# An earlier place for a bank's copy, and a pair's rounding in two pieces, in LSH attention with two feed-forward layers

## Chip, cores and metric

The kernel runs on one core of a Trainium2 chip. The metric is device time in microseconds (us) of one execution. The core has five engines that are used here: TensorE (PE, matmuls, with the weight loads shown apart as PEld), VectorE (DVE), ScalarE (ACT), GpSimd (POOL) and SyncE (SP, which issues DMAs). Each works through its own list of instructions in order and waits on semaphores for the others.

## What is computed

The input is q, k and v of 2 batches, 8 heads, 768 positions and 64 dimensions. Attention is masked by a hash: only positions whose six projection signs agree see each other. Two feed-forward layers follow. Cut to what matters:

```python
mask = q_bucket[:, :, :, None] == k_bucket[:, :, None, :]
scores = np.where(mask, scale * (q @ k.T), -1e9)
attn = exp(scores - scores.max(-1)) / sum
x = (attn @ v)                                   # (1536 tokens, 512)
x = (1/(1+exp(-(x @ w_gate))) * (x @ w_val)) @ w_out
h = x @ w_in2; y = (h * cos(h)) @ w_out2
```

## The kernel before, in words

Precision is kept by splitting: a value is rounded (the high part) and what the rounding left is subtracted out (the low part); matmuls run on the parts in turn.

The attention runs over 96 steps `g` (16 heads of 6 row tiles of 128 rows), plus nine steps in which the pipeline empties. In step `g` PE makes the scores of tile g+2 (`scores`, L451 and L454), DVE the row extremum of tile g+1 (`rowmax`, L462), ACT the exponential of tile g with its row sum (`expo`, L469), and POOL normalises tile g-3 (`norm`, L502). Seven steps behind (`LAG`), P is transposed on PE in blocks of three 128x128 (`ptrans`, L518), two blocks a step, called a and b. ACT rounds each block (`phi`, L523, orders HIa and HIb), DVE subtracts (`plo`, L528, LOa and LOb), and PE multiplies both parts with the values (`pv`, L538 with the high part, L539 with the low one). Six blocks fill one output bank `o`: a group `u`, half a head. There is one bank `o`, so the first `pv` of a new group waits until ACT has copied the bank out (`fin_act`, L548). Group u ends in step g = 3u + 10; at such a step the a block's `pv` (PVaF) stands late in the list.

Every third step `coef` makes the reciprocals of three tiles' row sums on DVE (L495), which `norm` uses. At the odd steps after a head's transposes its parts `x` pass through ACT (L301) and POOL (L302, L305). The values are split on POOL, too (`values`, L265, L268).

After the copy, DMAs on SP bring the halves of the output to their partitions (L550 to L562). For every pair of heads (u = 3, 7, ... 27, and at the end u = 30 and 31) POOL sums them three steps later (`fin_sum`, L575), and five steps later ACT rounds the sum into `xy` (`fin_hi`, L591) and POOL subtracts (`fin_lo`, L595). `xy` is held in tiles of 512 tokens, so the 768 tokens of a pair fall into two pieces: 512 and 256 in the first batch, 256 and 512 in the second.

Within a step, the order of work on all engines is written out by hand in `ORDER` (L21): each name stands for one operation, and each engine's list is what of the names falls to it. FIN is the end of a group (`finish_group`, L710: the copy, its DMAs and the entries for the later steps), PREP runs what is entered for this step (`run_todo`: loads, transposes of a coming head, `bits`, values, `fin_sum`, `fin_hi`, `fin_lo`), LATE what the step before left, W the first weights of the feed-forward part (from step 72), S the scores. In the last steps the order is the same list with COEF and NRM first (`LAST`). Behind the attention stand the matmuls of the feed-forward layers (L789, L851, L878).

Of the kernel before, what the change touches and what calls it, by code (L numbers as in the profile page):

```python
# [18 lines left out]
P = 128  # L19

ORDER = (  # L21
    "Tb LOa COEF NRM PVb EXP Ta MIN LATE W HIb PVa PREP S FIN HIa PVaF LOb".split()
)
LAST = ["COEF", "NRM"] + [name for name in ORDER if name not in ("COEF", "NRM")]
FILL = "COEF NRM MIN EXP LATE W PREP S".split()
# [6 lines left out]
SUM_AT, HIGH_AT, LOW_AT = 3, 5, 5  # L32
# [8 lines left out]
def lsh_attention_glu_moe_cos_moe(  # L41
# [14 lines left out]
    B, H, S, D = q.shape  # L56
# [5 lines left out]
    NH = B * H  # L62
# [164 lines left out]
    def attention():  # L227
        nonlocal done
        parts = None
        with ExitStack() as st:  # L230
# [10 lines left out]
            NG = NH * T  # L241
# [3 lines left out]
            def load(hd, nm, t0=0, t1=T, eng=nc.sync):  # L245
                b, h = divmod(hd, H)
                if nm == "v":
                    raw[hd, "v"] = nat.tile([P, 2, T * D], F32, tag="nv", name=f"nv{hd}", bufs=1)
                    nc.sync.dma_start(
                        raw[hd, "v"], v[b, h : h + 2].rearrange("h (p t) d -> p h (t d)", p=P)  # L250
                    )
                    return
                if hd not in raw:
                    raw[hd] = nat.tile([P, T, 2 * D], F32, tag="nqk", name=f"nqk{hd}")
                i = "qk".index(nm)
                eng.dma_start(
                    raw[hd][:, t0:t1, i * D : (i + 1) * D],
                    (q, k)[i][b, h].rearrange("(p t) d -> p t d", p=P)[:, t0:t1, :],
                )
# [304 lines left out]
            def fin_cols(u):  # L564
                if u // 2 < NH - 1:
                    return 0, S
                return u % 2 * HS, (u % 2 + 1) * HS

            def fin_engine(u):
                return nc.vector if u == 2 * NH - 1 else nc.gpsimd  # L570
# [6 lines left out]
            def pieces(u):  # L577
                b, h = divmod(u // 2, H)
                lo, hi = (b * S + c for c in fin_cols(u))
                c0 = lo  # L580
                while c0 < hi:
                    c, o = divmod(c0, 512)
                    n = min(512 - o, hi - c0)
                    yield xy[c][:, 0, h // 2, o : o + n], xy[c][:, 1, h // 2, o : o + n], f_t[u // 4][
                        :, c0 - b * S : c0 - b * S + n
                    ]
                    c0 += n

            def fin_hi(u):
                for h, _, x in pieces(u):  # L590
                    nc.scalar.copy(h, x)  # L591

            def fin_lo(u):
                for h, lw, x in pieces(u):
                    fin_engine(u).tensor_tensor(out=lw, in0=x, in1=h.bitcast(F32), op=ALU.subtract)  # L595

            LAG = 7
# [7 lines left out]
            def at(step, fn):  # L605
                todo.setdefault(step, []).append(fn)
# [42 lines left out]
            def run_todo(step):  # L649
                for fn in todo.pop(step, []):  # L650
                    e = fn()
                    if e is not None:
                        late.append(e)

            with tc.manual_schedule(
                engines={
                    mybir.EngineType.PE,
                    mybir.EngineType.Activation,
                    mybir.EngineType.DVE,
                    mybir.EngineType.Pool,  # L660
                    mybir.EngineType.SP,
                }
            ):
                for t0 in (0, 3):
                    load(0, "q", t0, t0 + 3)
                    load(0, "k", t0, t0 + 3, eng=nc.scalar)
                constants()
                for ps in s_ps:
                    nc.vector.memset(ps[:, :, HS : HS + 1], CUT)
                for g in range(2):  # L670
                    (nc.sync, nc.scalar)[g].dma_start(pj[D * g : D * g + D, :], proj)
                load(1, "k")
                load(1, "q")
                for g in range(2):
                    nc.sync.dma_start(
                        bcode[D * g : D * g + D],
                        xy[NC - 1]
                        .bitcast(F32)[0:1, 0, 0, 0 : 2 * D]
                        .rearrange("p (d two) -> p d two", two=2),
                    )  # L680
                load(2, "k")
                load(2, "q")
                load(0, "v")
                bit_weights()
                rest = first_head()
                split = [trans(1, half, fast=True) for half in range(2)]
                for high, _ in split:
                    high()
                place(1, 0)
                rest()  # L690
                scores(0)
                scores(1)
                rowmax(0)

                def first_low():
                    for _, low in split:
                        low()
                    place(1, 1)

                late.append(first_low)  # L700
                at(1, lambda: bits(1)())
                values(0)
                values(1)
                run_todo(-2)
                run_todo(-1)
                for g in range(NG + LAG + 2):
                    wa, wb = 2 * (g - LAG), 2 * (g - LAG) + 1
                    fin = (wb - 2) // T if 0 <= wb - 2 < NW and (wb - 2) % T == T - 1 else None

                    def finish_group():  # L710
                        fin_act(fin)
                        if fin % 4 == 3 or fin == 2 * NH - 2:
                            at(g + SUM_AT, lambda u=fin: fin_sum(u))
                            at(g + HIGH_AT, lambda u=fin: fin_hi(u))
                            at(g + LOW_AT + (3 if g < NG <= g + LOW_AT else 0), lambda u=fin: fin_lo(u))

                    def early_weights():
                        nonlocal done, parts
                        if g in WL:
                            load_to(1 + WL.index(g), nc.scalar)  # L720
                        if done < NEARLY and g >= WC and (g - WC) % WSTEP == 0:
                            parts = convert_parts(order[done])
                        if parts is not None and next(parts, parts) is parts:
                            parts = None
                            done += 1
                        elif parts is None and 0 < done <= NEARLY:
                            load_to(done + 3, nc.scalar)

                    def norms():
                        for n in range(g - 3, NG if g == NG else g - 2):  # L730
                            norm(n)

                    live_a, live_b, live_g = 0 <= wa < NW, 0 <= wb < NW, g < NG
                    third = 0 < g <= NG and g % 3 == 0
                    ops = {
                        "PVb": (0 <= wb - 2 < NW, lambda: pv(wb - 2)),
                        "FIN": (fin is not None, finish_group),
                        "Tb": (live_b, lambda: ptrans(wb)),
                        "LOa": (live_a, lambda: plo(wa)),
                        "EXP": (live_g, lambda: expo(g)),  # L740
                        "PVa": (live_a and fin is None, lambda: pv(wa)),
                        "MIN": (g + 1 < NG, lambda: rowmax(g + 1)),
                        "HIb": (live_b, lambda: phi(wb)),
                        "Ta": (0 <= wa + 2 < NW, lambda: ptrans(wa + 2)),
                        "COEF": (third, lambda: coef(g // 3 - 1)),
                        "LOb": (live_b, lambda: plo(wb)),
                        "NRM": (0 <= g - 3 <= NG - 3, norms),
                        "LATE": (True, run_late),
                        "W": (True, early_weights),
                        "S": (g + 2 < NG, lambda: scores(g + 2)),  # L750
                        "PVaF": (live_a and fin is not None, lambda: pv(wa)),
                        "PREP": (True, lambda: run_todo(g)),
                        "HIa": (0 <= wa + 2 < NW, lambda: phi(wa + 2)),
                    }
                    for name in ORDER if LAG - 1 <= g != NG else LAST if g == NG else FILL:
                        on, fn = ops[name]
                        if on:
                            fn()
                for step in sorted(todo):
                    run_todo(step)  # L760
# [214 lines left out]
```

## Time and profile before

| | |
|---|---|
| median of three runs | 801.71 us (801.66 to 801.79) |
| profiled execution, its own time | 801.66 us |
| its span in the trace | 799.9 us |
| PE busy | 788.9 us (99%) |
| DVE busy | 508.9 us (64%) |
| ACT busy | 469.8 us (59%) |
| POOL busy | 321.9 us (40%) |

Busy shares are taken over the whole span; in the attention, which takes the first 245 us or so, all engines are much busier than in the rest. Matmuls are pipelined: a matmul that stood waiting is shown longer than one in a dense row, so a wait of PE is seen in the length of a piece of the chain of waits rather than in idle time.

### The profile page before, as it was taken

Reading aid. Unit: us, or ns where it says so; the run is one execution under the profiler, and the core shown is the slowest. Engines: PE = TensorE matmul, PEld = TensorE weight load, DVE = VectorE, ACT = ScalarE, POOL = GpSimd, SP = SyncE. Lnnn points to the kernel's source line nnn. Section 1 sums busy time; section 2 is a strip of 40 time slices with the busy share of each in tenths; the row PEclk is TensorE's granted clock in tenths of the full one; section 3 lists DMA queues with packets and bytes.
Section 4 is the critical chain, followed back from the end, with each engine's and each line's share of the span. In section 5 each row is a group of like instructions: output and inputs, shape, how many; then the busy total and the mean of one; then the engine's idle time right before and its main releaser. Section 6 shows DMA issues by size and latency. Waiting matters only on the chain.

```text
span 799.9 us, 11617 instructions
## 1 busy us (share of the span) xinstructions
PE 788.9 (99%) x3984; PEld 677.4 (85%) x3984; DVE 508.9 (64%) x796; ACT 469.8 (59%) x932; POOL 321.9 (40%) x343
## 2 busy tenths in 40 slices
PE   6999999999999999999999999999999999999998
PEld 5999999999988888888888888888888888888886
DVE  7888888888986443334443266657655666676662
ACT  7999989989985332322232244456666656664442
POOL 5779989988871222222222112221222122222221
PEclk9999999999999999999999999999999999999999
DMA  7866675587413333222221122323223333242312
GB/s 171 203 154 144 159 184 147 135 212 193 112 51 100 123 119 102 79 79 79 80 79 53 53 73 86 113 73 116 93 82 105 106 106 103 82 158 81 105 53 105
DMA packets 70746, 89.03 MB, mean 111 GB/s; under 512 B 30112, under 2 KB 54816, under 8 KB 70688
## 3 DMA queue, kind: packets, MB, share of 16 engines
q1 hardware_dynamic: 67504, 85.43, 37.4%
q10 hardware_dynamic: 3184, 2.87, 1.3%
q8 instruction: 31, 0.51, 0.3%
q14 instruction: 27, 0.22, 0.1%
HBM read 59.77 MB, written 3.15 MB: 79 GB/s over the span
## 4 chain that ended last, share of the span: by engine, by line
PE 97%; ACT 1%; DVE 1%; DMA 0%; issue 0%; SPq 0%; DVEq 0%; ACTq 0%
PE a L878 16%; PE ph L789 16%; PE pg L789 12%; PE pv L789 12%; PE a L851 12%; PE t L518 8%; PE o L538 4%; PE o L539 4%; PE s L451 4%; PE s L454 4%; PE pb L342 2%; PE pt L284 1%; ACT p L469 1%; DMA pj<-in_proj 0%; DVE mn L462 0%
## 5 line engine op out<-in xcount | busy, mean ns | idle before, releaser
L789 PE MATMUL ph<-xy,ih 128*128 128x512 f32 x384 | 118.1, 389 | 0.0
L123 ACT CAST gh<-g 128x512 fp32r<-128x512 f32 x84 | 52.0, 620 | 109.4 <-PE a L878 43.7
L528 DVE TENSOR_TENSOR pl<-t,ph 128x384 fp32r<-128x384 f32 x192 | 102.9, 552 | 16.7 <-ACT ph L523 14.7
L124 POOL TENSOR_TENSOR zl<-w_z,zh 128x512 fp32r<-128x512 f32 x32 | 41.5, 1297 | 166.7 <-ACT zh L123 166.7
L502 POOL TENSOR_SCALAR p<-p,r,d 128x768 f32<-128x768 f32 x96 | 95.0, 995 | 22.0 <-PE t L518 9.9
L523 ACT CAST ph<-t 128x384 fp32r<-128x384 f32 x192 | 90.9, 486 | 17.6 <-PE t L518 16.2
L815 DVE TENSOR_TENSOR g<-pv,sg 128x512 f32<-128x512 f32 x36 | 24.9, 692 | 119.3 <-PE pv L789 119.3
L462 DVE TENSOR_REDUCE mn<-s 128x1 f32<-128x770 f32 x96 | 91.1, 950 | 13.0 <-PE s L454 11.9
L518 PE MATMUL t<-ident,p 128*128 128x128 f32 x576 | 94.8, 272 | 0.2 <-DVE bf L326 0.2
L124 DVE TENSOR_TENSOR gl<-g,gh 128x512 fp32r<-128x512 f32 x84 | 57.8, 688 | 53.0 <-ACT gh L123 50.7
L469 ACT ACTIVATE p<-s,mn 128x768 f32<-128x768 f32 x96 | 88.2, 919 | 2.7 <-DVE mn L462 2.4
L789 PE MATMUL pg<-xy,gh 128*128 128x512 f32 x288 | 89.3, 390 | 0.0
L789 PE MATMUL pv<-xy,vh 128*128 128x512 f32 x288 | 88.7, 389 | 0.0
L813 ACT ACTIVATE sg<-pg 128x512 f32<-128x512 f32 x36 | 21.4, 593 | 112.2 <-PE pg L789 112.2
L789 PEld LDWEIGHTS ph<-xy,ih 128*128 128x128 f32 x384 | 72.0, 188 | 14.9
L518 PEld LDWEIGHTS t<-ident,p 128*128 128x128 f32 x576 | 74.6, 140 | 8.4 <-POOL p L502 0.8
L538 PE MATMUL o<-ph,vs 128*128 128x384 f32 x192 | 79.2, 412 | 0.3 <-ACT e L548 0.3
L878 PE MATMUL a<-zh,gl 128*128 128x512 f32 x192 | 74.8, 390 | 0.0
L878 PE MATMUL a<-zl,gh 128*128 128x512 f32 x192 | 74.7, 389 | 0.0
L878 PE MATMUL a<-zh,gh 128*128 128x512 f32 x192 | 74.7, 389 | 0.0
L789 PE MATMUL ph<-xy,il 128*128 128x512 f32 x192 | 74.7, 389 | 0.0
L451 PE MATMUL s<-k,q 96*128 96x384 f32 x192 | 69.1, 360 | 2.9 <-ACT p L469 2.5
(111 smaller groups left out, 1738.2 us busy)
## 6 DMA issues: line engine op xcount, KB each, us to landing
raw_z<-in_moe_w_out SPq DMA_DIRECT2D x32, 512.0 KB, 3.3
raw_o<-in_moe_w_out SPq DMA_DIRECT2D x23, 512.0 KB, 3.3
q<-x SPq DMA_DIRECT2D x45, 192.0 KB, 3.6
k<-x SPq DMA_DIRECT2D x45, 192.0 KB, 3.8
raw_i<-in_moe_w_in SPq DMA_DIRECT2D x16, 512.0 KB, 4.0
raw_g<-in_moe_w_gate SPq DMA_DIRECT2D x10, 512.0 KB, 3.6
raw_v<-in_moe_w_val SPq DMA_DIRECT2D x10, 512.0 KB, 3.5
nv<-in_v SPq DMA_DIRECT2D x8, 384.0 KB, 4.2
```

Source lines behind the costliest of these rows:

```text
L124: sub.tensor_tensor(out=dst_l, in0=src, in1=dst_h.bitcast(F32), op=ALU.subtract)
L451: nc.tensor.matmul(o, hh["q2"][0:96, t, :], hh["k2"][0:96, sl, :], start=True, stop=False)
L462: nc.vector.tensor_reduce(mn_t[u][:, i : i + 1], s_t[g][:, :, 0 : HS + 1], axis=AX.XY, op=ALU.min)
L469: nc.scalar.activation(pt, s_t.pop(g)[:, :, 0:HS], AF.Exp, bias=mn_t[u][:, i : i + 1], scale=-1.0, accum_out=sm_t[u][:, i : i + 1],)
L502: nc.gpsimd.tensor_scalar(out=pt, in0=pt, scalar1=r[:, i : i + 1], scalar2=d[:, i : i + 1], op0=ALU.mult, op1=ALU.add,)
L518: nc.tensor.transpose(pt[:, i, :], pv_[:, j * P : (j + 1) * P], ident)
L523: nc.scalar.copy(ph, pt_t[w])
L528: nc.vector.tensor_tensor(out=pl, in0=pt_t.pop(w), in1=ph_t[w].bitcast(F32), op=ALU.subtract)
L538: nc.tensor.matmul(o_t[u], vs[:, j, :], ph_t.pop(w), start=(j == 0), stop=False)
L789: nc.tensor.matmul(ps, w[:, kt, :], xy[c][:, hl, kt, :], start=(n == 0), stop=(n == 11))
L851: nc.tensor.matmul(acc[c, e], w[:, e, :], m, start=(f == 0 and n == 0), stop=(f == F1 - 1 and n == 2),)
L878: nc.tensor.matmul(acc[c, t], m[:, ts], w, start=(f == 0 and n == 0), stop=(f == F2 - 1 and n == 2),)
```

## The change

In `ORDER`, FIN moves from behind S to behind W: the copy of a finished bank and its DMAs now stand ahead of HIb, the `pv` of block a, PREP and S. In `LAST`, which is made from `ORDER`, it moves as well. The lists of the other operations stay as they are.

`fin_hi` and `fin_lo` take a slice of the pieces. For pairs before the last one (u < 28) they are entered twice, for the first piece as before and for the second piece one step later.

```diff
-    "Tb LOa COEF NRM PVb EXP Ta MIN LATE W HIb PVa PREP S FIN HIa PVaF LOb".split()
+    "Tb LOa COEF NRM PVb EXP Ta MIN LATE W FIN HIb PVa PREP S HIa PVaF LOb".split()
...
-            def fin_hi(u):
-                for h, _, x in pieces(u):
+            def fin_hi(u, part):
+                for h, _, x in list(pieces(u))[part]:
                     nc.scalar.copy(h, x)
 
-            def fin_lo(u):
-                for h, lw, x in pieces(u):
+            def fin_lo(u, part):
+                for h, lw, x in list(pieces(u))[part]:
                     fin_engine(u).tensor_tensor(out=lw, in0=x, in1=h.bitcast(F32), op=ALU.subtract)
...
                             at(g + SUM_AT, lambda u=fin: fin_sum(u))
-                            at(g + HIGH_AT, lambda u=fin: fin_hi(u))
-                            at(g + LOW_AT + (3 if g < NG <= g + LOW_AT else 0), lambda u=fin: fin_lo(u))
+                            apart = fin < 2 * NH - 4
+                            for n, part in enumerate((slice(0, 1), slice(1, None)) if apart else (slice(None),)):
+                                at(g + HIGH_AT + n, lambda u=fin, part=part: fin_hi(u, part))
+                                at(
+                                    g + LOW_AT + n + (3 if g < NG <= g + LOW_AT else 0),
+                                    lambda u=fin, part=part: fin_lo(u, part),
+                                )
```

## Rows read from the trace of the kernel before

**Rows 1.** The page, part 4: shares of the chain that ended last.

```profile
PE 97%; ACT 1%; DVE 1%; DMA 0%; issue 0%; SPq 0%; DVEq 0%; ACTq 0%
```

**Rows 2.** Stretch, length; busy us: PE, PEld, DVE, ACT, POOL; clock, DMA share, GB/s.

```profile
60.00:103.00 43.00, 43.00 (x289) 40.66 (x288) 37.29 (x63) 39.79 (x94) 39.34 (x48) 1.00 0.61 147
...
245.00:800.00 555.00, 551.06 (x2431) 455.70 (x2429) 300.86 (x426) 250.99 (x425) 121.67 (x93) 1.00 0.29 93
```

**Rows 3.** Chain of waits, whole span, pieces in time: start us, us, what.

```profile
63.22 0.47 PE t L518 x3
66.80 0.39 PE o L538
...
181.25 0.40 PE o L538
```

**Rows 4.** Chain of waits from 200 to 245 us.

```profile
203.20 0.18 PE o L538
...
203.55 0.33 PE t L518 x3
...
216.56 0.44 PE o L538
...
228.91 0.44 PE o L538
```

**Rows 5.** Timeline at u = 5: start, us, engine, line, [idle before, releaser].

```profile
63.36 0.14 PEld L518 LDWEIGHTS t<-ident,p 128*128 128x128 f32 x1 [0.16 <-POOL p L502]
...
65.43 0.34 PE L539 MATMUL o<-pl,vs 128*128 128x384 f32 x1
...
66.18 0.52 ACT L548 COPY e<-o 128x384 f32<-128x384 f32 x1
...
66.75 0.19 PEld L538 LDWEIGHTS o<-ph,vs 128*128 128x128 f32 x1 [0.27 <-ACT e L548]
```

**Rows 6.** Timeline at u = 3 and the two steps behind it, four engines.

```profile
51.15 0.34 PE L539 MATMUL o<-pl,vs 128*128 128x384 f32 x1
51.23 0.48 ACT L523 CAST ph<-t 128x384 fp32r<-128x384 f32 x1
...
51.60 0.48 ACT L548 COPY e<-o 128x384 f32<-128x384 f32 x1
51.74 0.56 DVE L528 TENSOR_TENSOR pl<-t,ph 128x384 fp32r<-128x384 f32 x1
...
52.35 0.93 ACT L469 ACTIVATE p<-s,mn 128x768 f32<-128x768 f32 x1
...
53.22 0.34 PE L539 MATMUL o<-pl,vs 128*128 128x384 f32 x1
...
54.10 1.02 DVE L528 TENSOR_TENSOR pl<-t,ph 128x384 fp32r<-128x384 f32 x2 [0.17 <-ACT ph L523]
...
55.04 0.17 DVE L495 RECIPROCAL r<-sm 128x3 f32<-128x3 f32 x1
...
55.40 0.98 POOL L502 TENSOR_SCALAR p<-p,r,d 128x768 f32<-128x768 f32 x1 [1.09 <-PE t L518]
```

**Rows 7.** Timeline at the last copy, u = 31.

```profile
242.87 0.34 PE L539 MATMUL o<-pl,vs 128*128 128x384 f32 x1
...
243.24 0.48 ACT L548 COPY e<-o 128x384 f32<-128x384 f32 x1 [1.26 <-PE o L539]
```

**Rows 8.** Timeline at step 85: transposes, and scores behind them.

```profile
208.36 0.49 PE L518 MATMUL t<-ident,p 128*128 128x128 f32 x3
...
209.06 0.44 PE L451 MATMUL s<-k,q 96*128 96x384 f32 x1 [0.22 <-ACT p L469]
```

**Rows 9.** Timeline at step 27: the last normalisation of a group, its transposes' loads.

```profile
69.19 1.00 POOL L502 TENSOR_SCALAR p<-p,r,d 128x768 f32<-128x768 f32 x1
...
70.13 0.42 PEld L518 LDWEIGHTS t<-ident,p 128*128 128x128 f32 x3
```

**Rows 10.** All waits: engine line waited for, us in total, times, longest us.

```profile
PEld o L538 <- ACT e L548: 2.8, 9, 0.6
```

## Prediction

> **What bounds the kernel now.** I read the chain of waits first. TensorE (PE) carries 97% of it [rows 1], and in the feed-forward part PE is busy 551.06 of 555.00 us [rows 2]. Nothing in the change touches that part, so what it can win or lose is time in which PE stands still during the attention, up to about 245 us. That stretch is tight everywhere: between 60 and 103 us PE is busy all 43 us, ACT 39.79 and POOL 39.34 [rows 2]. A busy PE hides short waits, though, since a matmul that waited is shown longer. So the second reading is the chain's own pieces: an unhindered first matmul of `pv` takes 0.18 us and three transposes take 0.33 [rows 4], and every piece that is longer is a wait.
>
> Two kinds repeat with a period of 28.6 us (five pieces from 66.80 to 181.25), which is 12 steps, so a step is 2.38 us. One is the first matmul of a new group at 0.39 to 0.41 us, these five [rows 3]: 0.22 us too long each. It waits for the bank: PEld stood 0.27 us for the `e` copy [rows 5]. These are the ends u = 5, 9, 13, 17, 21. The other is the transposes of a new group at 0.47 us, 0.14 too long, first at 63.22 [rows 3]; the loader waited 0.16 us for POOL's normalised P [rows 5]. This one comes 12 steps apart too, six times, after the ends u = 3, 7, 11, 15, 19, 23. Singles come later: `pv` 0.44 at 216.56 (u = 26) and at 228.91 (u = 28) [rows 4], and around u = 25 scores that wait for the exponential: their end, 209.50, is 0.65 us behind the end of the transposes before, 208.85, where 0.18 is normal, so 0.47 too long [rows 8]. All in all there are only some 4 us to win before 245 us.
>
> **The copy moves ahead of HIb.** ACT runs its list in order. At an end it has the exponential, HIb (`ph`), the `e` copy, HIa (`ph`) and the next exponential, spaced 0.37 us: 51.23, 51.60, and two instructions on 52.35 [rows 6]. Swapped, the `e` copy could go at HIb's place, but it needs the last matmul of the group, which PE runs behind HIb's transposes. What does a copy cost that ACT reaches early? The last copy of all shows it: it sat idle 1.26 us and started at 243.24, 0.03 us after the shown end of its matmul (242.87 + 0.34 = 243.21) [rows 7]. The Trainium skill ("TensorE: Matmul & The Clock Gate", section "The cost: per-tile semaphore tail") models a signal behind one matmul at 25 + 4.7 + 26.3 = 56 ns; no run here shows its origin apart. By it the six losses below would be 0.02 us larger each, about 0.1 us in all; the measured 0.03 decides.
>
> At u = 3 the matmul ends at 51.15 + 0.34 = 51.49, so the copy starts at 51.52 instead of 51.60: it wins only 0.08 us. HIb follows 0.37 later, at 51.89 instead of 51.23, HIa at 52.27, and the next exponential at 52.64 instead of 52.35 [rows 6]. Here PE had no wait for the bank, so there is nothing to win, and ACT is 0.29 us late. The same swap at an even u happens before a step with six `pb` matmuls on PE, which leave ACT idle afterwards; I cost it at nothing (if that cover were gone: 0.29 for each of 15).
>
> Who waits for the late ACT? HIb's `pl` on DVE, at 51.74, would go to 52.40 (51.89 + 0.48 + 0.03) and end at 52.96; PE wants it at 53.22 [rows 6], so 0.26 us are left, enough. The other follower is not covered: behind the exponential come the row sums, two `ph`, two `pl` on DVE (54.10, idle 0.17 for ACT), the reciprocal at 55.04, and POOL's normalisation, which starts at 55.40, 0.19 after the reciprocal's end [rows 6]. POOL had been idle 1.09 us before it, and from there works without a pause through a head's parts, the values and the pair's sum up to the normalisation that releases the transposes, which are 0.14 late already. So each 0.29 us on ACT at u = 3 arrives undiminished at PE at 63.36: six times 0.29 = **+1.74 us**. Bounds: 0 if the row names the releaser rightly (a rival, below), 0.36 each (+2.2) if a waiting copy costs 0.10 instead of 0.03.
>
> **The wait for the bank at u = 5, 9, 13, 17, 21.** The group's last matmul ends at 65.43 + 0.34 = 65.77 [rows 5], or 0.29 later by the above: 66.06. The copy starts at 66.09, ends 0.49 to 0.52 later at about 66.60, and PE, whose scores now run until 66.53 + 0.29 = 66.82 (66.75 less the 0.22 it waited, plus 0.29), no longer waits. Gain 5 x 0.22 = **-1.12 us**, the sum of the five taken from the ends of the matmuls; bounds 0.9 to 1.2.
>
> **The split.** It adds and removes no arithmetic: the same casts on ACT and the same subtractions on POOL, seven pairs, the second piece one step later. At u = 3 the 512-wide piece stays and the 256-wide one moves behind HIb of the next end; from u = 19 on the wide one moves. ACT gets back about 0.3 to 0.5 us ahead of the exponential of that end, but there the copy must wait for PE, so the time is not kept. On POOL the order becomes piece, normalisation, two parts, piece, normalisation instead of both pieces first; the sum up to the normalisation at 69.19 is the same. It ends at 70.19, and the last of the three loads that begin at 70.13 comes some 0.28 later, at 70.41, and needs it 0.05 before [rows 9]: 0.17 to 0.22 us are left. In the new kernel POOL is 0.29 late and PE 0.29 - 0.22 = 0.07 late, so it just about fits. I take 0; bounds 0 and 0.2 for each of five.
>
> **Around u = 25 and later.** At step 84 the wide piece no longer stands before the exponential whose end PE awaits at 209.06; that 0.47 goes, and so do the 0.26 at 216.56 [rows 4, 8]. But weight conversions share ACT here and the moved 0.5 us comes back one step later, in front of the next exponential. Between nothing and 1.0 us I take half: **-0.5 us**. At u = 28 the copy follows an exponential and is held by its matmul: 0.08 us won, as at u = 3. With the ends behind it **-0.1 us** (0 to -0.5).
>
> **DMA queue.** The copies' transfers (SP) now stand ahead of the `q` load at odd ends; what queues behind is needed five steps, 11.9 us, later. No cost, and 0.6 us or so of lateness if it had no cover.
>
> **Sum:** +1.74 - 1.12 - 0.5 - 0.1 = 0.0 us on the profiled execution's 801.66 (span 799.9 and 1.76 around it); the median is 801.71. I say 801.7. With the bounds: 1.3 - 1.2 - 1.0 - 0.5 = -1.4 to 2.2 - 0.9 = +1.3, and up to 1.0 more if POOL's pieces don't fit.
>
> **The rivals.** *Bank only.* The profile names a PE transpose as releaser of the normalisation at 55.40 [rows 6], not the reciprocal. If that holds, POOL's train doesn't move with ACT, the 1.74 us vanish, and 801.7 - 1.74 = 799.9 us remain, faster by 0.22%. Against it: the normalisation reads the reciprocal, and starts right behind it. The Trainium skill ("PSUM — Partial Sum Buffer", "Summary: rules for kernel authors") says to evacuate promptly; by that alone all waits for this copy would go, 2.8 us on the loader in nine waits [rows 10], and the time would be 798.9. The trace agrees at nine of 32 ends; at the rest the bank is not what PE waits for. Together 20%.
>
> *POOL's pieces.* The slower side: the normalisation at 69.19 gets later by more than the 0.2 us that are left, because POOL's second piece now stands directly before it. It decides from 0.3 us: with 0.33 lost at each of five ends it costs 1.65 us, and the time is 803.4. For it: POOL is busy 39.34 of 43 us [rows 2]. Against it: the work is the same and the casts it needs are done two microseconds earlier. 13%.
>
> *The swap does nothing,* because ACT waits for the same matmul either way: true at most ends (0.08 us), but the bank waits at u = 5 show an ACT that is 0.41 us late (66.18 against 65.77), so not there. It gives 801.7, too; 3%.
>
> **How the numbers follow.** The forecast has 64%, its own range 800.3 to 803.0. Measurement of this kernel can tell about 0.2%, 1.6 us, from no change. Faster: the 20% of the first rival. Slower: 13% and the forecast's upper edge, 14%. Same: 66%. The range reaches down to the first rival and leaves the other out: 799.7 to 803.0.
>
> **What would show it.** Right: the first matmul of `pv` in the chain back at 0.18 us at the five ends; the transposes before them at about 0.76 instead of 0.47 us; reciprocal and normalisation after u = 3 0.3 us later than now against PE. Wrong: transposes still at 0.47 (then the first rival), a new wait at the transposes of steps 27, 39, 51 (then the second), or waits of PE for `pl` after the ends, which would mean that the 0.26 us of cover were not there.

## The result and the profile after

The changed kernel takes 805.78 us (median of six runs, 805.66 to 807.32), the kernel before beside it 801.69 us (801.58 to 802.10): a ratio of 1.0052, interval 1.0041 to 1.0062. It is slower by 4.1 us; the forecast was 801.7 (799.7 to 803.0), no change. The profiled execution took 805.66 us against 801.66.

The page of the changed kernel, the shares of the chain (part 4), against [rows 1]:

```profile
PE 89%; POOL 5%; DVE 2%; ACT 1%; DMA 1%; issue 1%; SPq 0%; POOLq 0%; ACTq 0%; DVEq 0%
```

The span grew by 4.0 us, from 799.9 to 803.9, and the chain now leaves PE for POOL and DVE: these engines are late for PE at more places. The list of waits of the changed kernel (engine, line waited for: us in total, times, longest us):

```profile
ACT e L548 <- PE o L539: 9.6, 29, 1.3
...
PEld o L539 <- DVE pl L528: 2.6, 5, 1.3
PEld t L518 <- POOL p L502: 2.5, 6, 0.4
PEld t L518 <- DVE pl L528: 2.2, 6, 0.7
PE o L539 <- DVE pl L528: 1.3, 2, 1.0
...
PEld o L538 <- ACT e L548: 1.2, 3, 0.5
```

The same lines of the kernel before:

```profile
ACT e L548 <- PE o L539: 1.3, 1, 1.3
...
PEld t L518 <- POOL p L502: 0.8, 5, 0.2
...
PEld o L539 <- DVE pl L528: 0.5, 2, 0.3
...
PEld t L518 <- DVE pl L528: 0.2, 1, 0.2
```

The wait that the earlier copy takes away fell from 2.8 us in nine times [rows 10] to 1.2 in three. In its place ACT stands 9.6 us in 29 waits for the last matmul of a group, and three waits of PE grew: for POOL's normalised P (L502), for `pl` ahead of transposes (L518), for `pl` ahead of `pv` (L539).

Times of one kernel scatter by up to about 2 us (the kernel before from 801.52 to 803.46 on one chip). The profiled execution of e1 below is 1.64 us behind that of the kernel before by step 12 (about 33 us); its granted TensorE clock was 0.50 (1.2 GHz) from 18.9 to 22.3 us, while every other profiled execution shows 1.00 (2.4 GHz) for its first 33 us. So stretches are compared below from step 12 on. So counted, the changed kernel is behind the one before by 1.30 us at the first `pv` after u = 21 (181.65 us before), by 2.30 after u = 27 (223.25), by 4.16 at the last `pv` (243.20) and by 3.92 at the end; up to step 12 by 0.08. The feed-forward part neither makes nor repairs it: 0.18 of the 4.16 are the place of one feed-forward matmul, which runs ahead of the last `pv` here and behind it in the kernel before. The same holds in e8, e12 and e13 below, and for two such matmuls in e2.

### The profile page after: what moved, and what is told of

Its sections match the earlier page's. It is cut to its first block, busy times and chain, and to the rows that moved or that the text cites. A ratio compares the mean times of both kernels' runs of the same rounds, so it can differ in the third digit from the quotient of the medians.

```text
span 803.9 us, 11579 instructions
## 1 busy us (share of the span) xinstructions
PE 790.1 (98%) x3984; PEld 677.9 (84%) x3984; DVE 507.8 (63%) x796; ACT 470.4 (59%) x932; POOL 321.0 (40%) x343
## 4 chain that ended last, share of the span: by engine, by line
PE 89%; POOL 5%; DVE 2%; ACT 1%; DMA 1%; issue 1%; SPq 0%; POOLq 0%; ACTq 0%; DVEq 0%
PE a L883 16%; PE ph L794 16%; PE pg L794 12%; PE pv L794 12%; PE a L856 12%; PE t L518 6%; PE o L539 3%; PE o L538 3%; PE s L451 3%; PE s L454 3%; POOL p L502 2%; POOL ef L575 1%; PE pb L342 1%; PE pt L284 1%; POOL vs L268 1%; DMA e<-e 1%
## 5 line engine op out<-in xcount | busy, mean ns | idle before, releaser
L528 DVE TENSOR_TENSOR pl<-t,ph 128x384 fp32r<-128x384 f32 x192 | 100.0, 551 | 26.8 <-ACT ph L523 24.6
L123 ACT CAST gh<-g 128x512 fp32r<-128x512 f32 x84 | 52.1, 620 | 109.2 <-PE a L883 43.7
L124 POOL TENSOR_TENSOR zl<-w_z,zh 128x512 fp32r<-128x512 f32 x32 | 41.5, 1296 | 167.0 <-ACT zh L123 167.0
L502 POOL TENSOR_SCALAR p<-p,r,d 128x768 f32<-128x768 f32 x96 | 94.5, 989 | 24.3 <-PE t L518 16.8
L518 PE MATMUL t<-ident,p 128*128 128x128 f32 x576 | 95.6, 273 | 1.8 <-POOL p L502 1.1
L523 ACT CAST ph<-t 128x384 fp32r<-128x384 f32 x192 | 87.0, 486 | 12.7 <-PE t L518 11.9
L124 DVE TENSOR_TENSOR gl<-g,gh 128x512 fp32r<-128x512 f32 x84 | 57.8, 688 | 53.1 <-ACT gh L123 50.9
L518 PEld LDWEIGHTS t<-ident,p 128*128 128x128 f32 x576 | 74.4, 140 | 11.8 <-POOL p L502 2.5
```

The source lines that it names most:

```text
L124: sub.tensor_tensor(out=dst_l, in0=src, in1=dst_h.bitcast(F32), op=ALU.subtract)
L502: nc.gpsimd.tensor_scalar(out=pt, in0=pt, scalar1=r[:, i : i + 1], scalar2=d[:, i : i + 1], op0=ALU.mult, op1=ALU.add,)
L518: nc.tensor.transpose(pt[:, i, :], pv_[:, j * P : (j + 1) * P], ident)
L523: nc.scalar.copy(ph, pt_t[w])
L528: nc.vector.tensor_tensor(out=pl, in0=pt_t.pop(w), in1=ph_t[w].bitcast(F32), op=ALU.subtract)
```

## Experiments

Each wait below is how much longer a matmul ran, by the ends of successive matmuls, than the same one in a dense row. "By u = 21" and "by the last `pv`" are the stretches just told, against the kernel before; each kernel's median stands beside that of the kernel before from the same chip. In the kernels that treat some ends differently, FIN stands in the list twice, behind W as `FINE` and at its old place as `FIN`, and a condition says which of the two runs.

### Which part costs what: e1, e2

**e1: the order alone,** on the kernel before.

```diff
-    "... MIN LATE W HIb PVa PREP S FIN HIa PVaF LOb"
+    "... MIN LATE W FIN HIb PVa PREP S HIa PVaF LOb"
```

> The copy ahead of HIb at all ends, the pair's casts and subtractions undivided. Theory (ACT is late at the ends, and POOL's train carries it to PE): transposes of a group at step 24 and its five like keep the 0.40 us wait of the changed kernel, the bank waits stay gone, but the wait of the transposes after step 26 (0.23 us, 0.57 once) goes, because the second cast no longer stands behind the waiting copy: 1.5 us less than the changed kernel, 804.2 us (803.7 to 804.6). The 1.28 us that PE waits for pl at 233 us stay. Rival (the split is harmless, the swap alone makes the loss): 805.7 us.

Measured: 804.70 us beside 801.82, ratio 1.0033 (1.0021 to 1.0046); +0.47 by u = 21, +2.60 by the last `pv`.

**e2: the split alone,** the changed kernel with the order of before.

```diff
-    "... MIN LATE W FIN HIb PVa PREP S HIa PVaF LOb"
+    "... MIN LATE W HIb PVa PREP S FIN HIa PVaF LOb"
```

> The casts and subtractions in two steps, the copy at its old place. Theory: ACT does the same work up to the copy of the next end, so the bank wait of 0.22 us and the 0.14 us of the transposes stay: 801.7 us, perhaps 0.4 less around step 85 (801.2 to 801.9). Rival (POOL's second piece directly ahead of a normalisation is what costs): 1.6 us more, 803.3 us.

Measured: 801.97 us beside 801.82, ratio 1.0000 (0.9992 to 1.0009); +0.09 by u = 21, +0.42 by the last `pv`, -0.06 at the end.

The waits of e1, then of e2 (columns as above):

```profile
ACT e L548 <- PE o L539: 8.4, 23, 1.3
...
PEld o L539 <- DVE pl L528: 2.5, 4, 1.3
PEld t L518 <- POOL p L502: 2.5, 6, 0.4
...
PEld t L518 <- DVE pl L528: 0.4, 2, 0.3
```

```profile
PEld o L538 <- ACT e L548: 3.7, 10, 0.6
```

So the split costs nothing by itself that can be measured here (-0.06 us), and the order alone brings two of the three grown waits: those for POOL's P and those for `pl` ahead of `pv`. The third, for `pl` ahead of transposes, is 2.2 us in the changed kernel and 0.4 in e1: most of it needs order and split together. e1 is near its expectation, which asked for 2.5 us more than before.

### Which ends: e4, e3, e11

**e4: the early copy only at u = 3, 7, 11, ...,** **e3: only at u = 1, 5, 9, ...,** **e11: only at even u below 28;** no split in any.

```diff
+    "FINE": (fin is not None and fin % 4 == 3, finish_group),                # e4
+    "FINE": (fin is not None and fin % 4 == 1, finish_group),                # e3
+    "FINE": (fin is not None and fin % 2 == 0 and fin < 28, finish_group),   # e11
```

> The copy ahead of HIb only at the ends u = 3, 7, ... 31; casts undivided. Theory: the six waits of the transposes at step 24 and its like grow from 0.14 to 0.40 us (+1.6), and since PE then comes later to the next end, the five bank waits close by themselves (-1.1): 802.2 us (801.8 to 802.6). Rival 1 (waits add): 803.3 us. Rival 2 (POOL's train hangs on PE and not on ACT): 801.7 us, transposes at 0.14.

Measured: 803.04 us beside 801.82, ratio 1.0009 (1.0000 to 1.0018); +0.81 by u = 21, +1.18 by the last `pv`. The six waits of the transposes are 0.40 to 0.44 us. But the five waits for the bank, whose copies this kernel leaves at their place, are gone, too. The chain of waits of e4 at u = 5 (start us, us, what):

```profile
61.34 1.82 POOL ef L575
63.16 0.98 POOL p L502
...
64.19 0.33 PE t L518
...
67.63 0.17 PE o L538
```

The first `pv` of the group runs 0.17 us, where [rows 3] has 0.39: PE comes so late out of the transposes that the copy is done. The two waits stand in one line, and the 1.12 us that the forecast took for the early copy at u = 5 come by themselves once the wait ahead of them grows. The time is still above the expected 802.2: by u = 21 these two kinds of wait make +0.29 of the +0.81; the rest is small, at most 0.06 us at one matmul, half of it at the scores, and its cause stays open.

> The copy ahead of HIb only at the ends u = 1, 5, 9, ... 29, where PE waited for the bank; casts undivided. Theory: ACT comes to these copies after their matmul, so it loses nothing; the bank waits go (5 x 0.22 us and the like at u = 25), the transposes at step 24 stay at 0.14: 800.5 us (800.0 to 800.9). Rival (the swap makes ACT late wherever it is made): 801.7 us or more.

Measured: 801.40 us beside 801.82, ratio 0.9994 (0.9985 to 1.0003); -0.99 by u = 21, -0.62 by the last `pv`. With the cause at u = 3 left out the bank waits are won, as expected; 0.37 us go again later, most of it into a new wait of 0.23 us of transposes that end at 183.93, so that the expected 800.5 is missed.

> The copy ahead of HIb only at the even ends before u = 28; casts undivided. Theory: ACT loses 0.3 us at each of the 14, and gets them back while PE makes the six pb matmuls: 801.7 us (801.5 to 802.0), no wait in the chain that is not there before. Rival (ACT's loss counts everywhere): 14 x 0.2 to 0.3 us, 804.5 us or more.

Measured: 801.71 us beside 801.76, ratio 1.0001 (0.9992 to 1.0010); -0.05 by u = 21, -0.08 by the last `pv`. ACT stands 5.9 us in 14 waits for the matmul (1.3 of it at the last end, as in the kernel before), and PE loses nothing on balance: at even ends it is covered, but for u = 26, where a bank wait of 0.28 us goes and one of 0.29 for `pl` comes three microseconds later.

### Whether the waits stand in one line: e6, e9

**e6: the sum of a pair one step later,** on the kernel before, so that POOL is free for the normalisation behind it; **e9: the same, with e3's early copy** (below u = 28).

```diff
-SUM_AT, HIGH_AT, LOW_AT = 3, 5, 5
+SUM_AT, HIGH_AT, LOW_AT = 4, 5, 5
```

> The kernel before with the pair's sum on POOL entered four steps behind the end instead of three, that is behind the normalisation that releases the transposes of step 24. Theory (POOL's train from the reciprocal to that normalisation is what these transposes wait for): all six waits of 0.14 us go, 800.9 us (800.6 to 801.4). Rival (they wait for PE's or ACT's own order): 801.7 us.

Measured: 802.16 us beside 802.16, ratio 1.0005 (0.9997 to 1.0014); +0.25 by u = 21. The transposes wait no more (the line `PEld t L518 <- POOL` is gone), but the bank waits at the five ends grew from 0.22 to between 0.41 and 0.43 us, and the expected gain of 0.8 us did not come. The waits of e6 and its chain at u = 5, which now runs through ACT:

```profile
PEld o L538 <- ACT e L548: 3.8, 9, 0.6
```

```profile
63.92 0.40 ACT xy L591
64.32 0.38 ACT ph L523
64.70 0.68 ACT p L469
...
66.44 0.39 ACT e L548
...
66.87 0.45 PE o L538
```

> The kernel before with the copy ahead of HIb only at the ends u = 1, 5, ... 25, and the pair's sum one step later; casts undivided. Theory (the waits of the transposes and for the bank stand in one line, so taking one away moves PE into the other, and both must go at once): transposes at 0 wait and bank at 0 wait at all five places, 12-step period 28.3 instead of 28.6 us: 1.6 us less than before, 800.1 us (799.8 to 800.8). Rival (a third wait of the same line takes it back): 801.3 us, as with the copy alone.

Measured: 801.02 us beside 801.76, ratio 0.9990 (0.9981 to 0.9998); -1.00 by u = 21, -0.67 by the last `pv`. Both waits are gone, and a third appears at five places, 0.12 us for `pl`, so it wins no more than e3 by u = 21, and not the expected 1.6: the rival came true.

### The third wait: e12, e7, e5, e10, e14

**e12: the changed kernel with the old place at u = 3, 7, ... and at u = 28.**

```diff
-    "FIN": (fin is not None, finish_group),
+    "FINE": (fin is not None and fin % 4 != 3 and fin != 28, finish_group),
```

> The changed kernel with the copy at its old place at the ends u = 3, 7, ... 31 and 28. Theory: the transposes at step 24 return to 0.1 to 0.14 us, the wait at 233 us goes; at u = 5 the copy, freed from the second cast, now stands for its matmul, so the wait of the next-but-one step's transposes (0.23 us) stays: about as before, 802.1 us (801.7 to 802.6). Rival (the split costs on its own once the copy is early anywhere): 803.3 us.

Measured: 802.92 us beside 801.76, ratio 1.0013 (1.0005 to 1.0022); -0.15 by u = 21, +1.17 by the last `pv`. The transposes of step 24 and its likes wait only 0.10 to 0.13, and the third wait is untouched: 0.23 us four times and 0.57 once (`PEld t L518 <- DVE pl L528: 2.2, 6, 0.7`, as in the changed kernel). So it isn't a sequel of the late POOL at u = 3. The expected 802.1 is missed mainly by the fifth of these waits.

**e7: the second piece two steps behind the first** instead of one, on the changed kernel.

```diff
-    at(g + HIGH_AT + n, ...)
+    at(g + HIGH_AT + 2 * n, ...)      # LOW_AT likewise
```

> The changed kernel with the pair's second cast and subtraction two steps behind the first instead of one, so out of the step in which the copy waits. Theory (the second cast behind the waiting copy makes HIb of the following step late, whose pl holds the bank of the next transposes): the wait of 0.23 us at 70 us and its three like go, and the 0.57 us at 186 us: 804.2 us (803.8 to 804.7). Rival (POOL's piece directly ahead of a normalisation makes it): the same loss in another place, 805.7 us.

Measured: 805.43 us beside 802.16, ratio 1.0041 (1.0028 to 1.0054). By u = 21 it is +0.85 where the changed kernel is +1.30: the four waits of 0.23 are gone, though four scores now wait 0.05 to 0.07 us longer than before. The expected 804.2 did not come: of the fifth wait, 0.57, 0.45 stay in two pieces, and the wait for `pl` at 221.7 us, 0.33 in the changed kernel, is 0.57 here.

**e5: the copy behind HIb** instead of ahead of it, with the split; **e10: e5 with the pair's sum one step later; e14: e10 with the 512-wide piece first in both batches.**

```diff
-    "... MIN LATE W FIN HIb PVa PREP S HIa PVaF LOb"
+    "... MIN LATE W HIb FIN PVa PREP S HIa PVaF LOb"
...
-SUM_AT, HIGH_AT, LOW_AT = 3, 5, 5      # e10, e14
+SUM_AT, HIGH_AT, LOW_AT = 4, 5, 5
```

> The casts in two steps as in the changed kernel, but the copy directly behind HIb instead of ahead of it. Theory (what costs is ACT standing idle for the matmul, not the order as such): behind HIb the matmul is done, ACT never stands, and with the second cast out of the way the copy at u = 5 comes 0.3 us earlier than before, which closes the five bank waits; transposes at step 24 stay at 0.10 to 0.14: 1.1 us less than before, 800.6 us (800.2 to 801.2). Rival (POOL's second piece or the split casts cost by themselves): 802 us or more.

Measured: 801.44 us (lowest 801.23) beside 802.16 (lowest 801.64), ratio 0.9993 (0.9984 to 1.0001); -0.71 by u = 21, -0.48 by the last `pv`. The five bank waits go, as expected; over half of that is taken back, 0.40 us of it at the transposes behind the fifth end.

> Casts in two steps, the copy directly behind HIb, and the pair's sum one step later. Theory: as with the copy behind HIb, and the 0.15 us of the transposes go, too, if the copy still comes in time for a PE that is 0.15 us earlier: 800.8 us (800.4 to 801.3). Rival (ACT's line sets the pace): the bank waits come back by 0.15 us each, 801.4 us.

Measured: 800.92 us beside 801.76, ratio 0.9991 (0.9982 to 1.0000); -1.09 by u = 21, -0.90 by the last `pv`. With e14 it has the lowest median of all, 0.1% below the kernel before, at the edge of what the interval can tell. The waits of e10:

```profile
PEld o L538 <- ACT e L548: 1.6, 5, 0.6
...
PEld t L518 <- DVE pl L528: 1.3, 6, 0.5
ACT e L548 <- PE o L539: 1.2, 1, 1.2
```

> Casts in two steps, the copy directly behind HIb, the sum one step later, and in both batches the 512-wide piece first. Theory: with the narrow piece behind the copy at u = 21 the wait of 0.41 us shrinks to the 0.05 to 0.08 us of the other four: 800.5 us (800.2 to 800.9). Rival (the wait comes from another source, such as the weight loads of that stretch): 800.9 us, as without.

Measured: 800.91 us beside 801.72, ratio 0.9989 (0.9981 to 0.9998); -0.93 by u = 21. The wait at 183.5 us is 0.30 instead of 0.41, and nothing is won overall against e10.

Directly behind HIb the matmul that the copy needs is done: ACT waits for it once, at the last end, as in the kernel before, instead of 29 times. The bank waits fall to about 0.10 us in e10 (at u = 21 to nothing) and the third wait to between 0.05 and 0.08 at four ends, with the same split; at the fifth 0.41 stay.

### Behind u = 28: e8, e13

**e8: the changed kernel with the old place at u = 28 alone; e13: the changed kernel, but the sum of the pair u = 27 one step later.**

```diff
+    "FINE": (fin is not None and fin != 28, finish_group),    # e8
...
-    at(g + SUM_AT, lambda u=fin: fin_sum(u))                  # e13
+    at(g + SUM_AT + (fin == 27), lambda u=fin: fin_sum(u))
```

> The changed kernel with the copy at its old place at the end u = 28 alone. Theory: the low part of the first gate weights (DVE) then stands two places later in DVE's list, clear of POOL's sum, and takes 0.7 us instead of 1.93; PE's wait of 1.28 us for pl at 233 us goes: 804.5 us (804.1 to 804.8). Rival (late ACT makes that wait): 805.7 us.

Measured: 804.77 us beside 802.16, ratio 1.0036 (1.0024 to 1.0048); +3.17 by the last `pv` against the changed kernel's +4.16. The wait of 1.28 us is gone, a part of it comes back in others.

> The changed kernel with the sum of the pair that ends at u = 27 entered one step later, behind POOL's next normalisation; DVE's list is as in the changed kernel, so the gate weight's low part stays at its place. Theory (DVE's subtraction of two SBUF operands stands while POOL's instruction holds what both need): it then stands only until that normalisation ends, takes 1.2 us instead of 1.93, and PE's wait for pl shrinks from 1.28 to about 0.5 us: 805.0 us (804.7 to 805.4). Rival (its place in DVE's list makes it long): 1.93 us as before, 805.8 us.

Measured: 804.94 us beside 801.72, ratio 1.0045 (1.0032 to 1.0059); +3.32 by the last `pv`. PE's wait is 0.44 instead of 1.28 us. What this tells stands in the next section.

## Why the prediction was wrong

In the profiled execution the steps of the sum came out so, each from the ends of successive matmuls: transposes +1.58 (forecast +1.74), bank -1.12 (-1.12), split +1.63 (0), around u = 25 +0.03 (-0.5), u = 28 and behind +1.63 (-0.1). Together +3.75 of the 4.0 us; 0.08 more had come before step 12. So three terms failed: the split, taken at nothing, the half of the gains around u = 25 that was to stay, and u = 28. The sum of the lower bounds also used 1.3 for the transposes, where their own bounds were 0 and 2.2.

**Transposes: right in size and cause.** The six waits went from 0.13 to 0.145 each to 0.39 to 0.41. The timeline of the changed kernel at u = 3 (start us, us, engine, line; in brackets the idle time before and its releaser), to be laid beside [rows 6]:

```profile
51.24 0.34 PE L539 MATMUL o<-pl,vs 128*128 128x384 f32 x1
...
51.62 0.48 ACT L548 COPY e<-o 128x384 f32<-128x384 f32 x1 [0.22 <-PE o L539]
...
52.74 0.93 ACT L469 ACTIVATE p<-s,mn 128x768 f32<-128x768 f32 x1
...
55.41 0.17 DVE L495 RECIPROCAL r<-sm 128x3 f32<-128x3 f32 x1
...
55.78 0.99 POOL L502 TENSOR_SCALAR p<-p,r,d 128x768 f32<-128x768 f32 x1 [1.39 <-PE t L518]
```

The last matmul is 0.09 us later than before, as all was here, but the copy, which waits for it, sends the exponential from 52.35 to 52.74, and reciprocal (55.04 to 55.41) and normalisation (55.40 to 55.78) follow it. The profile again names a PE transpose as releaser of the normalisation. The first rival, which believed it, fell: e4 gives the same wait with this copy alone. Of a wait for several semaphores the row names only one.

**Bank: right in size, but no term of its own.** All five are gone. But e4 shows that they go without the copy's move, and e6 that they grow when the wait ahead of them is taken away. That I added the two terms did no harm here, since the move did both; for the price of a part alone it was wrong: e4 moves the copy at u = 3, 7, ... only, and by u = 21 its transposes cost 1.43 us, of which 1.14 come back at the bank.

**Split: wrong, and the largest step but one.** "I take 0" had bounds of 0 and 0.2 for each of five ends. The wait came just where the second rival put it, at the transposes of step 27 and its likes: 0.23, 0.23, 0.24, 0.23 and 0.57 us of transposes that end at 70.27, 99.19, 128.12, 157.04 and 186.41, and 0.13 of a `pv` matmul that ends at 184.70. The second rival's 1.65 us hit its size by luck, not its cause, POOL's second piece. The changed kernel's timeline from u = 5 to step 27:

```profile
66.17 0.48 ACT L548 COPY e<-o 128x384 f32<-128x384 f32 x1 [0.23 <-PE o L539]
66.54 0.48 ACT L523 CAST ph<-t 128x384 fp32r<-128x384 f32 x1
66.91 0.42 ACT L591 CAST xy<-ef 128x256 fp32r<-128x256 f32 x1
67.22 0.49 ACT L523 CAST ph<-t 128x384 fp32r<-128x384 f32 x1
67.59 0.93 ACT L469 ACTIVATE p<-s,mn 128x768 f32<-128x768 f32 x1
...
68.84 0.84 ACT L523 CAST ph<-t 128x384 fp32r<-128x384 f32 x2
69.33 1.02 DVE L528 TENSOR_TENSOR pl<-t,ph 128x384 fp32r<-128x384 f32 x2 [0.16 <-ACT ph L523]
69.54 0.98 POOL L502 TENSOR_SCALAR p<-p,r,d 128x768 f32<-128x768 f32 x1
69.94 0.31 PEld L518 LDWEIGHTS t<-ident,p 128*128 128x128 f32 x3 [0.33 <-DVE pl L528]
```

and of the kernel before, the same casts, subtractions and loads:

```profile
68.21 0.84 ACT L523 CAST ph<-t 128x384 fp32r<-128x384 f32 x2
...
68.70 1.02 DVE L528 TENSOR_TENSOR pl<-t,ph 128x384 fp32r<-128x384 f32 x2 [0.17 <-ACT ph L523]
...
69.44 0.43 PEld L518 LDWEIGHTS t<-ident,p 128*128 128x128 f32 x3
```

At an end the copy now stands 0.23 us for its matmul, and the second piece's cast (`xy`, at 66.91) stands behind it, ahead of the next exponential. The casts of step 26 start 0.63 us later (68.84 against 68.21), the subtractions too (69.33 against 68.70), while PE itself is only 0.15 behind, and the loader waits for DVE, not for POOL, whose order I had worked out. Why would transposes wait for `pl`? They don't read it; they write into the bank that `pl` reads. There are three such banks in the code, and in a step in which PREP takes one for a coming head the next block's transposes get the bank of Tb of the same step, which `pl` of step 26 frees late. That chain of banks is read from the code; that ACT's order is the cause is shown for the four ends: no early copy (e2) or no second cast behind it (e1), and the wait is gone; with the second cast two steps later (e7) it is gone, too; with the copy behind HIb (e5, e10) it is at most 0.08 us there. At the fifth end (0.57) it is not the whole account: 0.17 us come without the split (e1), 0.23 with the early copy at u = 1, 5, ... alone (e3), and 0.40 stay with the copy behind HIb (e5, e10); what makes those is open. My cover of 0.26 us for `pl` counted PE's use of the data and left out the bank that it frees.

**Around u = 25: both gains came, but not half of them was lost: all.** The wait of the scores at 209.06 us [rows 8] went from 0.48 us to nothing and that at 216.56 [rows 4] from 0.28 to 0.02, as forecast. But three `pv` matmuls with the low part wait longer for `pl`: 0.55 us instead of 0.25, 0.20 instead of none, 0.34 instead of 0.03. The changed kernel's timeline at the first, and of the kernel before the same DVE instruction:

```profile
211.00 0.99 POOL L502 TENSOR_SCALAR p<-p,r,d 128x768 f32<-128x768 f32 x1
211.10 1.44 DVE L160 SCALAR_TENSOR_TENSOR w_g<-wp_g,wl_g 128x512 int32<-128x512 int32 x1
...
213.06 0.44 PE L539 MATMUL o<-pl,vs 128*128 128x384 f32 x1 [0.29 <-DVE pl L528]
```

```profile
209.49 0.91 DVE L160 SCALAR_TENSOR_TENSOR w_g<-wp_g,wl_g 128x512 int32<-128x512 int32 x1
```

L160, a step of a weight's conversion that stands ahead of `pl` on DVE, takes 1.44 us instead of 0.91 beside POOL's normalisation. In e8, where only the end u = 28 differs, it takes 0.68 and this wait is gone, but 0.54 us come at three matmuls behind it. The third wait belongs to the early copy at u = 26: e11, which has this copy and no split, wins 0.28 us at the bank and loses 0.29 there. No run took the conversions away, so that they are what takes the time back is argued.

**u = 28 and behind: wrong, 1.73 us off.** Most of it is one wait, 1.28 us. The diff doesn't name its cause, and why the lists came out so stays open: with the copy moved, the lists of ACT and DVE have the rounding of the first gate weight (`gh`, `gl`, L123 and L124, work of the feed-forward part that fills in here) ahead of the copy and of two subtractions instead of behind them. The changed kernel's timeline from 230 us:

```profile
230.53 1.83 POOL L575 TENSOR_TENSOR ef<-e,ef 128x768 f32<-128x768 f32 x1
...
230.98 1.93 DVE L124 TENSOR_TENSOR gl<-w_g,gh 128x512 fp32r<-128x512 f32 x1
...
232.34 1.42 POOL L502 TENSOR_SCALAR p<-p,r,d 128x768 f32<-128x768 f32 x1
...
232.82 1.01 DVE L528 TENSOR_TENSOR pl<-t,ph 128x384 fp32r<-128x384 f32 x2
...
233.43 0.45 PE L539 MATMUL o<-pl,vs 128*128 128x384 f32 x1 [1.01 <-DVE pl L528]
```

and of the kernel before, where `gl` came later in the list and beside a small POOL instruction:

```profile
230.67 0.69 DVE L124 TENSOR_TENSOR gl<-w_g,gh 128x512 fp32r<-128x512 f32 x1 [0.84 <-ACT gh L123]
...
230.81 0.65 POOL L487 TENSOR_SCALAR d<-mn 128x3 f32<-128x3 f32 x1
```

The same subtraction takes 1.93 us instead of 0.69, while POOL's sum runs; it ends at 232.91, 0.55 after the sum's end at 232.36. `pl` waits behind it on DVE, and PE for `pl`. e13 takes the sum away from that place and leaves the lists of ACT and DVE there as they are:

```profile
231.09 1.09 DVE L124 TENSOR_TENSOR gl<-w_g,gh 128x512 fp32r<-128x512 f32 x1
...
231.61 2.26 POOL L575 TENSOR_TENSOR ef<-e,ef 128x768 f32<-128x768 f32 x1
...
232.71 0.44 PE L539 MATMUL o<-pl,vs 128*128 128x384 f32 x1 [0.17 <-DVE pl L528]
```

`gl` falls to 1.09 us, the sum, which now starts inside it, grows from 1.83 to 2.26, and PE's wait falls from 1.28 to 0.44. What stays is the early `gl` behind the normalisation that POOL now runs there in the sum's place; it ends 0.53 us after it. In e8 `gl` is back at its place, takes 0.83, and the wait is gone. So the early `gl` makes the wait, and when the POOL instruction that runs beside it ends sets how long it is.

**Even ends and the DMA queue: right.** e11 puts the first at nothing on balance, and PE's only waits for a DMA are those for the first load at the start (3.7 us, as before).

## What to carry to other kernels

A copy that is put earlier in an in-order list than its producer can be done doesn't run earlier; it makes everything behind it wait, here 9.6 us on ACT in 29 waits instead of 1.3 in one; whether PE pays for that differs from end to end (nothing on balance at the even ones, e11). Put it behind the last instruction that still covers the producer (e5 and e10: directly behind HIb, one wait). Before adding up waits, ask whether they stand in one line, because removing the first enlarges the second (e6: 0.22 to 0.42) and enlarging the first closes the second (e4); and follow a delayed instruction not only to who reads its result but to who writes next into the buffer that it frees.

## What the runs showed of the hardware

A DVE instruction with two SBUF operands and a POOL instruction that run at the same time hold each other up, and the profile shows it as long busy instructions, not as idle time. `gl`, which takes 0.69 us in the kernel before, took 1.93 in the changed kernel, begun 0.45 us into POOL's sum, and 1.09 in e13 and 0.83 in e8, begun during a normalisation; L160 took 1.44, 0.91 and 0.68 us in the changed kernel, the one before and e8. Where such an instruction was held, it ended 0.53 to 0.56 us after the POOL instruction under way did (0.55, 0.53 and 0.54 for `gl`, 0.53 and 0.56 for L160). The POOL instruction that comes next is long in its turn: the normalisation 1.42 us behind the sum instead of 0.98, the sum 2.26 in e13 instead of 1.83, and the 128x3 `d` 0.65 in the kernel before, where the changed kernel has it at 0.24. Which of the two is held does not always follow from the start that the profile shows: in e8 L160 began 0.11 us into a normalisation and kept its 0.68, while the normalisation took 1.50; why, no run shows.

The Trainium skill ("SBUF — State Buffer", section "Who interferes with whom") describes a port pair that the two engines share, taken by one for a whole instruction while the other is blocked, and names among the users a DVE instruction with two operands in SBUF beside a POOL instruction that reads SBUF. These runs agree: `gl` ended 0.55 us after the sum's end, and `pl`, one of whose operands is in PSUM, kept its time beside POOL (two in 1.01 us from 232.82, while the normalisation ran from 232.34 to 233.76).
